# Four blocks of 32 columns in place of two of 64, in the stretches of an FFN loop that have no convolution pairs beside them

## The chip, the cores and the metric

The kernel runs on one core of one Trainium2 chip. The metric is device time in microseconds (us) from one launch; three runs of the kernel before gave a median of 2205.84 us (2205.76 to 2206.69). All arithmetic is in fp32.

## What is computed

A long convolution by FFT, a multiplication, and a feed-forward network (FFN) with a maximum of three products. Cut to what matters:

```python
h_filt = (np.maximum(pos_emb @ w1, 0.0) @ w2) * np.exp(-0.01 * pos)[:, None]
u = x * v                                          # (4, 12544, 128)
Uf, Hf = np.fft.rfft(u, n=2 * S, axis=1), np.fft.rfft(h_filt, n=2 * S, axis=0)
y = np.fft.irfft(Uf * Hf[None], n=2 * S, axis=1)[:, :S]
t = (x * y).reshape(4 * 12544, 128)
h = np.maximum(np.maximum(t @ m1, t @ m2), t @ m3) # m1, m2, m3: 128 x 768
out = h @ m_out                                    # 768 x 128
```

## The kernel before

**Stages.** A prologue builds the filter's spectrum and the convolution of batch 0 (it ends near 284 us of the span). Then a main loop (lines 1264 to 1311) runs the FFN of batches 0, 1 and 2 and, beside it, the convolution of the next batch. A last stage (from line 1320, near 1792 us) runs the FFN of batch 3 with a Strassen-like scheme and nothing beside it.

**Tiles and slots.** A batch is 32 tiles of 392 tokens (4 positions by 98), and each tile takes 6 slots, one for each block of 128 of the 768 hidden columns. The main loop therefore has 3 x 192 = 576 slots. A slot issues, in this order: `up` (line 844, two products of a 128x128 weight block with 392 columns of tokens, each evicted by ScalarE or VectorE), perhaps `t_sums`, `down` of two slots before (line 855, one product, and one more with `lin` at the first block of a tile), in one slot of a tile `t_last` (line 825, the last stage of the inverse FFT of the next tile: eight products of 49 columns with a weight of 90 rows), and then `run(besides...)`, the steps of the next batch's convolution that the planner put in this slot. Line 1309 issues one `t_last` more near the end of the loop.

**The products' blocks.** `up`, `down` and `t_last` all go through `halves_mm` (line 164). It cuts the 128 columns of the stationary operand into blocks of `block[0]` columns, one matmul to each, and each block writes its own partitions of the output. `block` is 64 at line 162 and is set to 32 at line 1317, ahead of the last stage. So the main loop runs two blocks of 64 and the last stage four blocks of 32. In the trace, each fp32 matmul is two instructions (two passes), so a product of 392 columns is 4 MATMUL instructions with blocks of 64 and 8 with blocks of 32. The passes are issued in the order pass 1 of all blocks, then pass 2 of all blocks.

**What runs beside.** Two kinds of step of the next batch's convolution use TensorE. `u_two` (line 496) is the first stage of the FFT of two units: 64 instructions at line 451, on tiles of 49 rows by 64 columns. `g_quarter` (line 539) is what the change calls pairs: its instructions at lines 549 and 559 are on tiles of 64 rows by 64 columns. Both write other shapes of the array than the FFN's 128 rows by 64 columns.

**The planner.** `conv_steps` (line 669) spreads these steps over the slots. It places the units first (line 685, every `2 * UNIT * per_pair` slots), then the pairs: pair x starts at slot `s0 + int(x // 2 * 2 * per_pair)`, with x from 0 to 47. By lines 681 to 703, `per_pair` is 2.520 for the steps beside batch 0 and 2.542 for those beside batches 1 and 2, and `s0` is 60, 59 and 59. The last pairs start at slot 175 of each batch. Units run in slots 2 to 52 of a batch, and, for the batch after next, in slots 183, 187 and 191 of batches 0 and 1. The `plan` list holds the slots of `t_sums` and `t_last` for each tile.

**Queues.** SyncE issues the loads of the units, of the pairs and of the tiles `zt`; GpSimd issues weight loads, the stores `zd` and `out_dram`, and computes the units' products and planes. VectorE multiplies the result of `t_last` (line 839) into the tile that `up` reads in the next tile's slots.

## Time and profile before

| what | value |
|---|---|
| median of three runs | 2205.84 us |
| the profiled execution, its own time | 2205.64 us |
| its span, first to last instruction | 2203.9 us |
| PE busy | 2186.5 us (99%) |
| VectorE, ScalarE, GpSimd busy | 70%, 55%, 54% |
| mean granted TensorE clock | 0.999 |

"PE" is TensorE's matmuls, "PEld" its weight loads. The ends of matmuls are modelled, so in the timeline the starts are what counts: the distance from the start of one group to the start of the next is what the group takes on TensorE. A line of the timeline gives the start in us, the length, engine, source line, operation, the tiles' names (output from inputs), the array tile as rows*columns, the moving operand's size, and how many instructions were merged. Line 169 is the helper `halves_mm`, so the kind of product is read from the names: `hps<-gt,w_sb` is `up`, `ops<-hid,wo_sb` is `down`, `ops<-gt,lin` the product with `lin`, and `cps<-f4p` (`last<-f4p` in the last stage) is `t_last`.

### The profile page before, as it was taken

To read this page: it belongs to the slowest core of one execution; us is meant where nothing else is said; L and a number is where in the kernel's file an instruction comes from. 1 tells how busy PE (TensorE), PEld (TensorE's weight loads), DVE (VectorE), ACT (ScalarE), POOL (GpSimd) and SP (SyncE) were. 2 spreads that over 40 slices of the span, in tenths; PEclk is the share of its full clock that TensorE was granted. 3 is DMA by queue.
4 is the path that set the end of the run, shared out by engine and by line. 5 is a ranking of instruction groups with operands and counts; after the bars stand their busy time and mean duration, and the time that the engine had idled before them with its cause. 6 is when DMAs were issued, how large, how long until landed. Compare 5 with 4: busy or idle time off the path is not lost.

```text
span 2203.9 us, 77207 instructions
## 1 busy us (share of the span) xinstructions
PE 2186.5 (99%) x31655; PEld 1258.5 (57%) x31655; DVE 1533.7 (70%) x3292; ACT 1211.4 (55%) x2223; POOL 1183.3 (54%) x1580
## 2 busy tenths in 40 slices
PE   9999999999999999999999999999999999999998
PEld 8988855555555555555555455555555545555565
DVE  5688966678888766668888766668878745454443
ACT  3699845466666555466666555456666522222222
POOL 1166568545544667535455566534545326666665
PEclk9999999999999999999999999999999999999999
DMA  8789999879999899789999899879999622222221
GB/s 200 184 262 318 302 181 206 170 196 247 248 245 246 209 189 178 155 193 243 245 245 251 212 193 175 171 172 244 242 251 241 179 75 59 65 71 69 59 59 24
DMA packets 491270, 411.62 MB, mean 187 GB/s; under 512 B 289379, under 2 KB 407901, under 8 KB 490917
## 3 DMA queue, kind: packets, MB, share of 16 engines
q1 hardware_dynamic: 443495, 274.33, 57.5%
q0 software_dynamic: 45936, 130.43, 20.9%
q8 instruction: 249, 4.08, 0.8%
q10 hardware_dynamic: 1486, 1.93, 0.4%
q14 instruction: 104, 0.85, 0.1%
HBM read 262.85 MB, written 84.68 MB: 158 GB/s over the span
## 4 chain that ended last, share of the span: by engine, by line
PE 93%; DVE 2%; POOL 2%; issue 1%; DMA 0%; ACT 0%; POOLq 0%; ACTq 0%; DVEq 0%
PE hps L169 46%; PE ops L169 20%; PE ops L913 6%; PE cps L169 4%; PE cps L549 3%; PE cps L451 3%; PE ps L178 3%; PE cps L559 3%; PE ps L169 2%; POOL xt L640 1%; PE last L169 1%; DVE ab L647 1%; PE ps L393 1%; DVE xs L639 1%; POOL specH L640 1%
## 5 line engine op out<-in xcount | busy, mean ns | idle before, releaser
L169 PE MATMUL hps<-gt,w_sb 128*64 128x392 f32 (+1 forms) x7672 | 1151.8, 494 | 1.8 <-DVE hid L852 1.0
L849 ACT ACTIVATE hid<-hps 128x392 f32<-128x392 f32 x768 | 382.4, 498 | 745.2 <-PE hps L169 726.9
L169 PEld LDWEIGHTS hps<-gt,w_sb 128*64 128x64 f32 (+1 forms) x7672 | 413.7, 126 | 454.5 <-issue 415.9
L852 DVE TENSOR_TENSOR hid<-hid,hps 128x392 f32<-128x392 f32 x768 | 428.5, 558 | 339.9 <-PE hps L169 321.4
L169 PE MATMUL ops<-hid,wo_sb 128*64 128x392 f32 x2304 | 476.8, 492 | 0.0
L601 POOL TENSOR_TENSOR cb<-cb,xs 128x512 f32<-128x512 f32 x135 | 178.2, 1320 | 358.3 <-DVE xs L598 349.8
L169 PEld LDWEIGHTS ops<-hid,wo_sb 128*64 128x64 f32 x2304 | 165.7, 137 | 213.5 <-issue 213.5
L574 DVE TENSOR_TENSOR cb<-cps,eo 128x512 f32<-128x512 f32 (+1 forms) x288 | 175.2, 650 | 78.0 <-ACT eo L571 76.9
L867 POOL DMA_DIRECT2D out_dram<-ot x96 | 77.1, 803 | 263.6 <-ACT ot L865 247.3
L589 ACT ACTIVATE xs<-cb 32x512 f32<-32x512 f32 x270 | 169.5, 628 | 21.9 <-DVE cb L574 13.1
L590 ACT COPY xs<-cb 32x512 f32<-32x512 f32 x270 | 166.3, 616 | 3.1
L605 DVE TENSOR_TENSOR xs<-cb 128x256 f32<-128x256 f32 x270 | 148.3, 598 | 7.3 <-POOL cb L601 7.3
L431 ACT COPY uT<-turned 113x512 uint16<-113x512 uint16 x180 | 125.9, 770 | 1.9 <-DMA turned<-planes 1.7
L388 POOL TENSOR_TENSOR ut<-ut 128x392 f32<-128x392 f32 x90 | 92.8, 1032 | 43.1 <-DMA ut<-in_vr_dram 42.9
L582 POOL DMA_DIRECT2D zd<-cb x135 | 93.8, 695 | 39.9 <-DVE cb L574 36.8
L169 PEld LDWEIGHTS cps<-f4p,even 90*64 90x64 f32 x1552 | 87.2, 138 | 35.9 <-issue 33.1
L777 POOL DMA_DIRECT2D xT<-in_x_dram x172 | 101.4, 605 | 4.6 <-DVE ab L647 3.1
L473 DVE TENSOR_TENSOR low<-high,cps 128x180 f32<-128x180 f32 x186 | 54.7, 336 | 68.9 <-ACT high L463 68.9
L938 POOL DMA_DIRECT2D out_dram<-o x120 | 72.6, 610 | 45.6 <-DVE o L931 44.5
L169 PE MATMUL cps<-f4p,zt 90*64 90x49 f32 x1552 | 95.9, 222 | 0.0
L415 POOL COPY planes<-ut 128x392 uint16<-128x392 uint16 x180 | 94.9, 561 | 0.0
L169 PE MATMUL cps<-f4p,even 90*64 90x49 f32 x1552 | 94.6, 220 | 0.0
(173 smaller groups left out, 3306.1 us busy)
## 6 DMA issues: line engine op xcount, KB each, us to landing
ht<-hd SPq DMA_DIRECT2D x264, 256.0 KB, 6.8
wt<-wq_const POOLq DMA_DIRECT2D x144, 256.0 KB, 5.6
zd<-cb POOLq DMA_DIRECT2D x135, 256.0 KB, 5.1
zt<-zd SPq DMA_DIRECT2D x384, 90.0 KB, 3.8
sq<-spec SPq DMA_DIRECT2D x528, 64.0 KB, 5.9
ut<-in_xr_dram SPq DMA_DIRECT2D x128, 196.0 KB, 4.0
ut<-in_vr_dram SPq DMA_DIRECT2D x128, 196.0 KB, 4.3
wt<-wt_const SPq DMA_DIRECT2D x90, 256.0 KB, 5.1
```

The lines of the kernel that those rows point to most:

```text
L169: nc.tensor.matmul(out[h:h + w], lhsT[:, h:h + w], rhs, start=start, stop=stop, skip_group_check=True)
L415: nc.gpsimd.tensor_copy(w[:, h, :, :, 0:HB], a[:].bitcast(U16).rearrange("p s (m e h) -> p h s e m", e=2, h=2)[:, h])
L431: nc.scalar.copy(uts[u][0:HR, 8 * (u % 2):8 * (u % 2) + 8].rearrange("n s r t -> n (s r t)").bitcast(U16).rearrange("n (s r t h) -> n h s ...
L574: nc.vector.tensor_tensor(out=cb[:, a, lo:hi], in0=ps[:, lo:hi], in1=eo[:, lo:hi], op=op)
L589: nc.scalar.mul(xs[at:at + 32], xt[at + 32:at + 64], -1.0)
L590: nc.scalar.copy(xs[at + 32:at + 64], xt[at:at + 32])
L601: nc.gpsimd.tensor_tensor(out=xts[g], in0=xts[g], in1=xs[:], op=ALU.add)
L605: nc.vector.tensor_tensor(out=ab[:, q], in0=y[:, 0], in1=y[:, 1], op=(ALU.subtract, ALU.add)[q])
L777: eng.dma_start(xT[c * NG:(c + 1) * NG].rearrange("d i p n -> d (i p) n"), x[:, 4 * i:4 * i + 8, c, b, :])
L849: nc.scalar.activation(h[:], pa[:, 0:N], Relu)
L852: nc.vector.tensor_tensor(out=h[:], in0=h[:], in1=pb[:, 0:N], op=ALU.max)
L913: nc.tensor.matmul(ps[32 * q:32 * q + 32, 0:H2], w[:, m:m + 32], rhs[:, H2 * c:H2 * c + H2], start=start, stop=True, skip_group_check=True)
```

## The change

`conv_steps` also returns the slot two after the start of the last pair, which is 177 in all three batches, and the main loop sets the block size anew in each slot. Slots 0 to 59 (0 to 58 in batches 1 and 2) and 177 to 191 run `up`, `down` and `t_last` in four blocks of 32 columns; the slots between stay at two of 64. The last value is 32, so the first `up` of batch 3 and the two `down` after the loop (lines 1313 to 1315) also go to 32. The last stage had 32 already. The steps of the units and pairs do not use `halves_mm` and keep their shapes.

```diff
-        return slots, plan, s0
+        return slots, plan, s0, start(NK + LATE - 1) + 2
...
-            plan, pairs_from = plans[b]
+            plan, pairs_from, pairs_to = plans[b]
...
         for f in range(NF):
-
+            block[0] = 64 if pairs_from <= i * NF + f < pairs_to else 32
             if i < NT - 2:
```

## The prediction

> **What bounds the kernel now.** I read the page first, then TensorE's waits in the stretches that the change touches, then busy time by stretch, then the timeline. The page says that TensorE is the bound and carries the chain:

> ```profile
> PE 2186.5 (99%) x31655; PEld 1258.5 (57%) x31655; DVE 1533.7 (70%) x3292; ACT 1211.4 (55%) x2223; POOL 1183.3 (54%) x1580
> ...
> PE 93%; DVE 2%; POOL 2%; issue 1%; DMA 0%; ACT 0%; POOLq 0%; ACTq 0%; DVEq 0%
> ```

> A busy PE is modelled, so I asked for TensorE's waits in 290 to 436 us and 1740 to 1792 us, two stretches without pairs: none is listed in either. What counts there is the distance between starts, and a time saved on TensorE is saved in the span as long as the others keep up. Busy time by stretch (us, with instructions; clock, DMA share, GB/s at the end) for a stretch without pairs, one of the prologue and one of the last stage:

> ```profile
> 300.00:440.00 140.00, 140.00 (x1800) 72.76 (x1798) 91.78 (x271) 75.37 (x140) 96.37 (x144) 1.00 1.06 191
> 130.00:210.00 80.00, 80.00 (x1698) 71.41 (x1696) 71.30 (x190) 77.66 (x142) 53.54 (x70) 1.00 0.95 312
> 1860.00:1890.00 30.00, 30.00 (x596) 15.27 (x592) 13.87 (x26) 7.61 (x16) 20.84 (x25) 1.00 0.21 54
> ```

> In the first stretch GpSimd, the busiest of the others, has 96 of 140 us. The DMA engines are full there, which matters for a rival.

> The last stage already runs blocks of 32, so the trace shows both sizes. A stretch without pairs, in blocks of 64:

> ```profile
> 305.67 0.29 PE L169 MATMUL cps<-f4p,zt 90*64 90x49 f32 x4
> 305.79 1.50 PE L169 MATMUL hps<-gt,w_sb 128*64 128x392 f32 x8
> 307.12 0.83 PE L169 MATMUL ops<-hid,wo_sb 128*64 128x392 f32 x4
> 307.88 1.48 PE L451 MATMUL cps<-f1e,uT 49*64 49x90 f32 x64
> 309.29 1.54 PE L169 MATMUL hps<-gt,w_sb 128*64 128x392 f32 x8
> 310.66 0.83 PE L169 MATMUL ops<-hid,wo_sb 128*64 128x392 f32 x4
> ```

> The border of the two sizes, and `t_last` in blocks of 32:

> ```profile
> 1790.71 1.49 PE L169 MATMUL ops<-hid,wo_sb 128*64 128x392 f32 x8
> 1792.13 6.79 PE L169 MATMUL hps<-gt,w_sb 128*32 128x392 f32 x80
> 1798.74 0.27 PE L169 MATMUL last<-f4p,even 90*32 90x49 f32 x8
> ...
> 1822.55 0.27 PE L169 MATMUL last<-f4p,even 90*32 90x49 f32 x8
> 1822.64 0.27 PE L169 MATMUL last<-f4p,zt 90*32 90x49 f32 x8
> ...
> 1823.26 1.50 PE L169 MATMUL hps<-gt,w_sb 128*32 128x392 f32 x16
> 1824.58 0.52 PE L913 MATMUL ops<-hid,tw 128*32 128x196 f32 x8
> ```

> **The change, part by part.** How much is touched: 60 + 15 slots beside batch 0 and 59 + 15 beside batches 1 and 2 make 223 of 576. A `t_last` stands in slot 2, 3 or 4 of each tile; tiles 0 to 9 and 29 to 31 of a batch lie in those slots (13), times 3, and one more from line 1309: 40. Products of 392 columns: 223 x 3, one with `lin` for each of 12 tiles a batch (36), and 4 after the loop: 709. Visits to the units' products (line 451): all 46 lie in those slots.

> *`up` and `down`.* From the border on, 80 instructions are 5 `up`, or 10 products, in 1798.74 - 1792.13 = 6.61 us: 0.661 each, with what the switch costs in it. In blocks of 64, a slot without anything else takes 1.97 to 1.98 us in the timeline (1761.58, 1763.55, 1765.53), 0.658 a product. Single passes stand 329 ns apart in either size. The four blocks start a few ns apart and then stream side by side, as the two do. I take no difference. The upper end is the last stage's slot, one `up` and two half products in 1.98 us, or 0.660 a product: 709 x 0.0017 = 1.2 us lost. The lower end is 0: both sizes stream the same 392 columns twice.

> [...]

> *`t_last`.* In blocks of 64 it takes 0.92 us (timeline: 293.40 to 294.32, 1744.04 to 1744.96, 1756.69 to 1757.61), and the `up` behind it 1.33 (305.79 to 307.12) where an `up` otherwise takes 1.316. A product of 49 columns takes 0.115 us (305.67 to 305.79). In blocks of 32 it is 0.088 us, the whole `t_last` 0.71 (1822.55 to 1823.26; 0.70 at 1798.74 and 1905.73), and the `up` behind it 1.32. [...] The saving is 0.92 - 0.705 + 0.015 = 0.23 us, times 40 = **9.2 us**. Its input `zt` is ready without a wait on TensorE now, and `up` of that tile comes at least one slot later, so VectorE's multiplication at line 839 hides as before.

> *Switches of shape.* At the border the two `down` (1.316 us) should end at 1792.03, and the first `up` in 32 starts at 1792.13: 0.10 us. Five `up` then take 6.61 where 5 x 1.316 = 6.58: 0.03 more. So a switch from 64 to 32 costs about 0.13. The way from 64 to the units' tiles costs the same 0.10 (307.12 + 0.66 = 307.78, start at 307.88), and behind the units the `up` takes 1.37 (309.29 to 310.66), 0.05 over its due. The change adds one switch 64 to 32 and one 32 to 64 in each batch, and takes away the one at 1792.13: 3 x (0.13 + 0.15) - 0.13 = **+0.7 us**.

> *Units beside blocks of 32.* Each of the 46 visits now goes from 32 to 49x64 tiles and back. No row shows that pair of shapes. The switches in the rows above cost 0.10 to 0.13, whatever the two shapes, so I take the same for the way in. For the way back I take the 0.03 of the border in place of 0.05: 46 x -0.025 = **-1.1 us**. Bounds: -46 x 0.05 = -2.3 if the way back lost its extra; +46 x 0.10 = +4.6 if one more stall of the border's size came with each visit.

> *More instructions.* A slot gets 12 more MATMUL and as many weight loads, a `t_last` 32 and 32: 223 x 24 + 40 x 64 = 7,900 on top of the program's 77,207. I cost this at nothing: the prologue row above feeds TensorE 3,394 instructions in 80 us (42 a us) at a DMA share of 0.95 with PE busy throughout. The 300 to 440 stretch goes from 3,598 to some 5,500 (55 slots of 24 and 9 `t_last` of 64 more), 39 a us. If that cover is gone it is a rival.

> Sum: -9.2 + 0.7 - 1.1 + 0 = -9.6 us. The profiled execution, 2205.64 us with a span of 2203.9, becomes 2196.0; it lies 0.2 under the median of 2205.84, so the median becomes **2196.2 us** (-0.44%).

> **The rivals.**

> *A, slower: leaving and entering four column tiles is dear.* There are 92 switches between 32 columns and the units' tiles. From 0.10 us extra at each, the gain is gone (9.6 / 92); at 0.2 extra, one and a half times the dearest switch of the rows (0.13), they cost 18.4 us and the time is 2205.8 - 9.6 + 18.4 = 2214.6. For it: no row has this pair of shapes. Against it: three kinds of switch have one price. [...] 0.11.

> *B, slower: the instruction feed.* The feed shares the DMA engines, whose share is 1.06 in the stretch. It decides if TensorE is fed under 39 instructions a us. At 36, each such stretch of 140 us would need 5,500 / 36 = 153, and 3 of them cost some 40 us: 2245. Against it is the prologue's row. 0.03.

> *C, no change: the gain is given back as waits.* The units' transposes and loads fill the DMA engines, and GpSimd waits 15.4 us for `ut` loads in 290 to 440. If TensorE were paced by them, 2205.8. Against: TensorE shows no wait there, and the loads are issued up to 9 slots ahead, against a saving of 2.3 us in a stretch of 60 slots. 0.10.

> *D, a part of the gain:* the bounds of products and units fall to the dear side, or a product pays for starting two more blocks. With +1.2 for the products and +4.6 in place of -1.1 for the units: 2205.8 - 9.2 + 0.7 + 1.2 + 4.6 = 2203.1. With the border's 0.661 for every product (0.003 more, 2.1 us) and the rest as forecast: 2198.3. 0.12 in all, spread from 2198 to 2203. [...]

> **How the numbers follow.** My forecast has 0.64, within 2194.3 (the way back loses its extra, and a little more) to 2199. Its own range and D's to 2203.1 hold 0.76; to hold 0.8 the range goes a little into C, 2194.3 to 2205. A measurement can tell about 0.2% from no change, here 2201.4 to 2210.3. Faster by more: 0.64 and most of D, 0.73. Within: C, the rest of D and the mild half of A, 0.16. Slower: the rest of A, and B, 0.11.

> **What would show it.** In the profile after, `t_last` before 440 us should be rows of 90*32 with x8, 0.70 to 0.71 us from its first start to the next `up`; slots without side work should still take 1.97 to 1.98; the way from `down` to line 451 should still lose 0.10 and the `up` behind it take 1.34 to 1.37. The first pair of batch 0, at 441.65 us now, should come 2.3 us earlier (10 x 0.23), and the last stage some 9 us earlier. The prediction is wrong if the visits to line 451 take longer, if TensorE's weight loads wait for issue at the slots' starts, or if waits for VectorE or a DMA appear on TensorE in those stretches.

## The result, and the profile after

The changed kernel takes 2209.12 us (median of 20 runs, 2205.29 to 2215.47); the kernel before, on the same chips, 2206.98 (20 runs, 2205.30 to 2209.60). The ratio is 1.0013, 95% interval 1.0007 to 1.0019: not 9.6 us faster but some 3 us slower, outside the stated range. The runs also spread more than those of before. The profiled execution is the slowest of the 20 (2215.47 us, span 2213.7), so its account is not that of a typical run.

The page of the changed kernel, where it answers to the lines of before:

```profile
PE 2187.1 (99%) x35763; PEld 1267.0 (57%) x35763; DVE 1535.4 (69%) x3292; ACT 1213.1 (55%) x2223; POOL 1188.7 (54%) x1580
...
q8 instruction: 281, 4.60, 0.9%
...
PE 91%; POOL 3%; DVE 2%; issue 2%; DMA 2%; ACT 1%; POOLq 0%; SPq 0%; ACTq 0%; DVEq 0%
```

TensorE's busy time is the same, but its idle time grew from 2203.9 - 2186.5 = 17.4 us to 2213.7 - 2187.1 = 26.6, and the chain has a second percent of "issue", time in which an engine waits for nothing that the profile shows. Queue q8, of the kind `instruction`, moved 281 transfers; before it moved 249 (`q8 instruction: 249, 4.08, 0.8%`).

Where the time went is seen by cutting the span at the first and last instruction of each batch's pairs (lengths in us, from the starts in the traces; "free" is a stretch without pairs: free 0 from the first `up`, free 1 and 2 from the last pair of one batch to the first of the next; the 2 to 4 us ahead of the first `up` are left out; e3, e6a and e6b are told below):

```
                         before    after     e3    |   e6a     e6b
up to the first t_last   281.56   284.02   284.42  |  282.56  282.96
free 0                   157.73   165.19   157.94  |  157.73  155.99
pairs 0                  304.70   306.32   315.06  |  304.47  304.47
free 1                   196.35   197.34   196.62  |  196.51  193.73
pairs 1                  306.76   306.52   307.30  |  306.53  306.54
free 2                   196.35   193.65   196.62  |  196.49  193.74
pairs 2                  306.03   306.03   313.00  |  307.00  306.03
rest of batch 2           46.91    45.98    47.04  |   46.91   45.98
last stage               405.12   405.08   405.18  |  405.18  405.16
```

Free 2 went nearly as forecast, 2.70 us shorter, and so did the rest of batch 2. Free 0 is 7.5 us longer.

Not all of the 9.8 us between the two spans can be put down to the change. The 2.5 us ahead of the first `t_last` lie in code that is the same in both, and other kernels here with that same code took 281.6 to 284.4 for it. From there to the first `up` another 1.2 us came in, and behind it the granted clock is at 0.50 from 287 to 293 us, which makes the time from the first `up` to the next `t_last` 10.97 us in place of 9.48. This half clock comes without the change too: e3, with blocks of 64 in free 0, has it there, and so has e13 (told below), which is the kernel before up to the last stage:

```profile
287.00:290.00 3.00, 3.00 (x12) 1.22 (x10) 2.90 (x10) 0.58 (x2) 1.47 (x2) 0.50 0.79 199
```

The 1.6 us of pairs 0 hold one wait of 1.2 us for the input `sq` of a pair (at 691 us), in slots whose blocks are 64 in both kernels. Some 3 us are left for the rest of the loop. TensorE's timeline in free 0, changed kernel:

```profile
425.50 0.27 PE L169 MATMUL cps<-f4p,zt 90*32 90x49 f32 x7
426.73 0.23 PE L169 MATMUL cps<-f4p,zt 90*32 90x49 f32 x1 [0.97 <-issue]
426.74 0.31 PE L169 MATMUL cps<-f4p,even 90*32 90x49 f32 x8
...
429.39 1.31 PE L451 MATMUL cps<-f1e,uT 49*64 49x90 f32 x55
433.49 0.71 PE L451 MATMUL cps<-f1e,uT 49*64 49x90 f32 x9 [2.78 <-issue]
434.13 2.72 PE L169 MATMUL hps<-gt,w_sb 128*32 128x392 f32 x16
```

TensorE stops in the middle of a product: after 7 of 8 instructions of a `t_last` that need nothing but what the seven had, and after 55 of 64 of the units' products. No input can be late there. And the `up` behind the second stop takes 2.55 us instead of 1.32. The windows around it (us, TensorE's busy time and instructions first, then its weight loads, VectorE, ScalarE, GpSimd; granted clock, DMA share, GB/s at the end) say why:

```profile
424.00:430.00 6.00, 5.03 (x137) 2.64 (x133) 2.48 (x7) 0.99 (x2) 2.82 (x3) 1.00 1.06 239
430.00:434.00 4.00, 1.22 (x47) 0.96 (x36) 1.29 (x4) 0.46 (x1) 0.00 (x0) 0.90 0.62 168
434.00:437.00 3.00, 3.00 (x25) 0.91 (x24) 0.00 (x1) 0.96 (x2) 0.00 (x0) 0.57 0.02 5
```

After the stop the granted clock is 0.57. TensorE's waits in 290 to 442 us of the changed kernel, in total, times, longest; of before, none was listed there:

```profile
PE cps L451 <- issue: 2.8, 1, 2.8
PE cps L169 <- issue: 1.3, 2, 1.0
PE hps L169 <- issue: 1.1, 1, 1.1
```

**The instruction feed in the trace.** Before, TensorE ran 63,310 matmuls and weight loads; with the 601 instructions that wait for semaphores or drain, which are counted from here on, that is 63,911. Queue q8 has 249 transfers of 16 KB there, one for every 257, and the 8,216 that the change adds go with 32 more, again one for every 257. So I take q8 for TensorE's instructions, and a transfer for 256 of them. I set the start of each transfer against the count of TensorE's instructions started by then. In all profiles of this case, from 20 us on, no transfer n started before TensorE was 150 instructions past 256 n, and TensorE was never further than 449 past it before transfer n had landed. I read this as a store of instructions: a load is due at 150, and at 449 the store is empty. No view shows the store itself; the two counts are what was measured. Between them lie 299 instructions, and the time that they take is the time that a load has. Of the six gaps over 0.7 us between two instruction starts from 290 to 1800 us of the changed kernel, five stand at just this place (instruction 193 of a 256, 449 = 256 + 193), and TensorE went on 1.5 to 1.7 us after the transfer's end; the sixth is the wait for `sq`. Before has none there. Because of these 1.5 us a load cost time here also where it landed before the store was empty: of the five, two landed 0.03 and 1.55 us after that moment, the other three 0.4 to 0.9 us ahead of it. The times from due to landed, against the time in which TensorE uses up 299 instructions (us):

```
                            landed median / longest    store median / shortest
before, 288 to 440               3.07 / 8.31                11.38 / 10.56
after, 288 to 440                4.47 / 7.60                 7.89 /  4.33
before, prologue 130 to 210      3.93 / 5.37                 6.98 /  6.84
before, 1800 to 2195             1.94 / 3.43                 6.66 /  5.50
```

The longest landing and the shortest store need not belong to the same load, so each load has to be set against its own 299 instructions. With blocks of 64 in the main loop of before the closest load landed 3.5 us before its store was empty, and in the prologue 1.6 us (130 to 210). In the changed main loop seven landed with less than 1 us left or after it. The changed kernel uses up the store fastest where a `t_last` in blocks of 32 (64 matmuls and 64 weight loads in 0.70 us) stands near the units' products (128 in 1.41): 256 of the 299 are gone in 2.1 us.

### The profile page after: what moved, and what is told of

Read it like the earlier page. It is cut to its first block, busy times and chain, and to the rows that moved or that the text cites. A ratio compares the mean times of both kernels' runs of the same rounds, so it can differ in the third digit from the quotient of the medians.

```text
span 2213.7 us, 85423 instructions
## 1 busy us (share of the span) xinstructions
PE 2187.1 (99%) x35763; PEld 1267.0 (57%) x35763; DVE 1535.4 (69%) x3292; ACT 1213.1 (55%) x2223; POOL 1188.7 (54%) x1580
## 4 chain that ended last, share of the span: by engine, by line
PE 91%; POOL 3%; DVE 2%; issue 2%; DMA 2%; ACT 1%; POOLq 0%; SPq 0%; ACTq 0%; DVEq 0%
PE hps L169 46%; PE ops L169 20%; PE ops L913 6%; PE cps L169 4%; PE cps L549 3%; PE cps L451 3%; PE ps L178 3%; PE cps L559 3%; POOL xt L640 1%; PE ps L169 1%; PE last L169 1%; DVE ab L647 1%; PE ps L393 1%; DMA zt<-zd 1%; DVE xs L639 1%
## 5 line engine op out<-in xcount | busy, mean ns | idle before, releaser
L169 PE MATMUL hps<-gt,w_sb 128*32 128x392 f32 (+1 forms) x9464 | 1168.8, 496 | 2.5 <-issue 1.7
L169 PEld LDWEIGHTS hps<-gt,w_sb 128*32 128x32 f32 (+1 forms) x9464 | 420.2, 118 | 456.4 <-issue 412.7
L169 PE MATMUL ops<-hid,wo_sb 128*32 128x392 f32 (+1 forms) x3196 | 488.0, 492 | 0.0
L169 PEld LDWEIGHTS ops<-hid,wo_sb 128*32 128x32 f32 (+1 forms) x3196 | 162.7, 122 | 219.6 <-issue 218.8
L169 PEld LDWEIGHTS cps<-f4p,even 90*32 90x32 f32 (+1 forms) x2192 | 82.6, 121 | 37.5 <-issue 33.7
L593 DVE TENSOR_TENSOR cb<-cb,ht 128x512 f32<-128x512 f32 x135 | 92.1, 682 | 1.8 <-ACT xs L590 1.6
L598 DVE TENSOR_TENSOR xs<-xs,ht 128x512 f32<-128x512 f32 x135 | 92.0, 682 | 0.0
```

The source lines that it names most:

```text
L169: nc.tensor.matmul(out[h:h + w], lhsT[:, h:h + w], rhs, start=start, stop=stop, skip_group_check=True)
```

## The experiments

Theory F: TensorE uses up its instructions faster than they land. Rivals: N, the number of instructions costs by itself, wherever; K (and B32), blocks of 32 cost through clock, weights or switches.

**e1 and e2: the turning transfers left out**, at 64 and at 32. Both leave out the turning of the units, so the FFT's data of batches 1 to 3 is another.

```diff
-        nc.sync.dma_start_transpose(
-            out=t[:], in_=us.pop(u)[:].rearrange("p h s n -> p (h s n)"))
+        nc.sync.dma_start(out=t[:], in_=us.pop(u)[:].rearrange("p h s n -> p (h s) n"))
```

> This kernel has blocks of 64 as before, and leaves out the turning of the units: the DMA transposes at line 422 become plain copies of the same bytes, so the FFT of batches 1 to 3 gets unturned data. It is the base for the next kernel. Theory F (feed): in the changed kernel TensorE runs out of instructions, because their loads stand behind the transposes on full DMA engines; here, at blocks of 64, there is hardly such a stall, so the time stays within 4 us of before (2203 to 2208), and the DMA share near 300 to 440 us falls from 1.06 to under 0.6. Rival N (number alone: four blocks cost by their number of instructions, whatever the DMA engines do): the same here. Rival K (clock: blocks of 32 lower the granted clock): the same here.

> The changed kernel (32 where no pairs run) with the same left out: plain copies in place of the transposes. F: with the DMA engines free the instructions come in time, so no wait of TensorE for issue over 0.3 us is left between 290 and 1800 us, and the gain that the working of t_last gives comes through: 8 to 10 us less than e1_no_turn_64. N and K: 0 to 4 us more than e1_no_turn_64, as the change itself showed, and stalls or a lower clock remain.

Measured: 2208.45 (ratio to before 1.0005, 0.9997 to 1.0014) and 2203.96 (0.9988, 0.9979 to 0.9997): 4.5 us in favour of 32, where the change itself lost 2 to 3. That is against N and K, but half of what F expected. e2 still has four gaps at the store's end (0.73 to 1.37 us): its DMA share in 300 to 440 us is 0.78 (e1: 0.76, not under 0.6), and loads there still land up to 7.2 us after they are due.

**e6a and e6b: most of the units' transfers left out**, at 64 and at 32: no turning transfer, and one of a unit's two inputs (it is multiplied with itself).

```diff
-        for src in (xr, vr):
+        for src in (xr, vr)[:1 if b else 2]:
...
-        nc.sync.dma_start_transpose(
-            out=t[:], in_=us.pop(u)[:].rearrange("p h s n -> p (h s n)"))
-        us[u] = t
+        us[u] = us[u][:].rearrange("p h s n -> p (h s) n")
```

> Base for the next kernel: blocks of 64, and most of the units' transfers left out in batches 1 to 3: no turning transfer at all (the join reads the planes as they are), and only one of the two loads of a unit (it is multiplied with itself). Both theories: near before, 2202 to 2207.

> The changed kernel with the same transfers left out. F: the loads of instructions land sooner than in e2_no_turn_32, so more of the gain comes through, 7 to 10 us less than e6a_light_64 against 4.5 us between e2_no_turn_32 and e1_no_turn_64. B32: the same as that 4.5 us or less, since transfers do not matter.

Measured: 2207.83 (0.9994, 0.9985 to 1.0003) and 2199.44 (0.9965, 0.9951 to 0.9978), a difference of 8.4 us: nearly the whole gain that the prediction saw. The same 300 to 440 us, e6a and then e6b:

```profile
300.00:440.00 140.00, 140.00 (x1800) 72.77 (x1798) 91.21 (x270) 75.68 (x141) 91.25 (x144) 1.00 0.47 108
```

```profile
300.00:440.00 140.00, 139.68 (x2778) 66.74 (x2772) 91.78 (x271) 76.17 (x141) 92.63 (x144) 1.00 0.49 112
```

With the DMA share at half, e6b feeds 5,550 instructions in 140 us with 0.3 us of stop, and has no gap at the store's end over 0.7. From 288 to 440 us its loads land after 2.5 us in the median, against 4.5 in the changed kernel; the latest takes 7.2 us here too, but it met a stretch whose store lasted 8.0. By stretches without pairs it gains 1.74, 2.78, 2.75 and 0.93 us. TensorE's work is the changed kernel's, form by form; what differs is transfers. So it is neither the number of instructions alone (N) nor the blocks of 32 (K, B32).

**e3: the complement, 32 only beside pairs; e4: 32 from the first pair on.**

```diff
-            block[0] = 64 if pairs_from <= i * NF + f < pairs_to else 32
+            block[0] = 32 if pairs_from <= i * NF + f < pairs_to else 64   # e3
+            block[0] = 32 if pairs_from <= i * NF + f else 64              # e4
```

> The complement of the change: blocks of 32 only in the slots with pairs beside them (351 to 353 of 576, with 57 or 58 t_last), 64 where none run. F: TensorE needs 23.5 instructions a us there now and about 32 with blocks of 32, under the 37 to 40 at which the changed kernel stalled, and no transposes run there; few stalls, so 57 x 0.23 = 13 us less for t_last, 1 us more for switches: 2193 to 2197. N: more instructions are added than by the change (351 x 24 + 57 x 64 = 12,000 against 7,900), so 2209 to 2214. K: the same sign as N.

> Blocks of 32 from the first pair of a batch to its end, 64 only in slots 0 to 59 of each batch, where most units run. F: the gain of e3_beside_pairs and 2 us more (10 t_last x 0.23), 2191 to 2195, less if the units in slots 183 to 191 of batches 0 and 1 already starve TensorE. N and K: slower than before by more than the change, 2210 to 2216.

Measured: 2224.20 (1.0072, 1.0058 to 1.0085) and 2229.44 (1.0095, 1.0083 to 1.0108). F's numbers were wrong in sign. Its rule, an average of under 37 instructions a us, was the wrong rule: beside pairs e3's loads land a median of 5.4 and up to 8.7 us after they are due (450 to 740 us), while a `t_last` and a slot's pairs (up to 64 matmuls and 64 weight loads) empty the store in as little as 4.7. TensorE's four largest waits in 284 to 1800 us of e3, and one of the stops, 6 matmuls into a pair:

```profile
PE cps L559 <- issue: 5.7, 6, 1.9
PE hps L169 <- issue: 4.5, 3, 3.2
PE ops L169 <- issue: 3.9, 4, 1.4
PE cps L549 <- issue: 3.2, 3, 1.9
```

```profile
512.15 0.44 PE L549 MATMUL cps<-sq,wt 64*64 64x128 f32 x6
514.50 0.54 PE L549 MATMUL cps<-sq,wt 64*64 64x128 f32 x9 [1.91 <-issue]
```

All 14 gaps over 0.7 us from 290 to 1800 us in e3, and 15 of 17 in e4, stand at instruction 193 of a 256. The kind of stop is F's in every one of these. N had the sign, but not the size (2209 to 2214), and e6b is against it.

**e5: as many instructions without blocks of 32.** In the slots without pairs, `up` and `down` keep blocks of 64 and are cut into halves of 196 columns.

```diff
+        m = n // 2 if split[0] and n == 4 * NB else n
+        for c in range(0, n, m):
             for h in range(0, P, w):
-                nc.tensor.matmul(out[h:h + w], lhsT[:, h:h + w], rhs, ...
+                nc.tensor.matmul(out[h:h + w, c:c + m], lhsT[:, h:h + w], rhs[:, c:c + m], ...
```

> Blocks of 64 everywhere in the main loop, but in the slots without pairs each product of up and down is cut into two of 196 columns, so that these slots issue as many instructions for it (24 more) as with blocks of 32, and no block of 32 is in it. A pass of 196 columns takes 166 ns in the last stage against half of 329, which is 6 ns a product or 4 us in all. Theory F (TensorE runs out of instructions where it uses them faster than their loads land): 4 us for the products and some 6 to 10 us of stalls for issue in the same stretches as in the changed kernel, 2215 to 2222. Rival B32 (it is the blocks of 32 themselves, by their weights, switches or clock, that cost): only the 4 us, 2209 to 2212, and no waits for issue.

Measured: 2214.66 (1.0032, 1.0021 to 1.0043), between the two. In the profiled execution the stretches without pairs are 4.8 us longer, some 4 of it the price of the halves by the estimate above, and one gap (0.9 us) stands at the store's end. `t_last` keeps its 32 matmuls here, so the store lasts 6.7 us or more. It does not decide; it fits that the bursts matter more than the mean rate.

**e7: only the 40 `t_last` at 32.**

```diff
+        w, block[0] = block[0], 32 if narrow[0] else block[0]
         for s in range(4):
...
+        block[0] = w
```

> Only the 40 t_last of the slots without pairs go to blocks of 32; up and down stay at 64. F: 2,560 more instructions in place of 7,900, so few stalls; 40 x 0.23 = 9.2 us less for t_last, and 2 switches of 0.13 more for each, 10.4 us, come to about +1: 2206 to 2210. B32 (blocks of 32 cost as such, and with them every switch): 3 to 6 us over before.

Measured: 2210.23 (1.0012, 1.0003 to 1.0020), 2.3 us over before: just past F's upper end, and under B32's 3 to 6. No gap at the store's end. Free 1, with 13 `t_last`, is 0.57 us longer than before: 0.044 each, so if a `t_last` saves its 0.23, the two added switches cost 0.23 + 0.044 = 0.27 us, 0.137 each, and eat the saving. Free 0 is 2.8 us longer in this profile for another reason: two waits for `hid` at 332 and 336 us, behind a wait of ScalarE of 3.5 us for a turning transfer. So in this one profile a late transfer of data did hold up TensorE, which is rival C's way of losing time, though not with the changed kernel's blocks.

**e8, e9, e10: transfers added to the last stage**, which runs blocks of 32 without a stop. e8 adds loads of the units' form that nothing reads; e9 adds them with blocks of 64 in that stage; e10 has the blocks of 64 alone.

```diff
+            if 12 <= step < 168:
+                for src in (xr, vr):
+                    t = inp.tile([P, 4, NB], FP32, tag="u0" if src is xr else "u1", name="junk")
+                    nc.sync.dma_start(t[:], src[...])
```

> The kernel before, with transfers added where there were few: in steps 12 to 167 of the last stage SyncE also issues two loads of 196 KB each, of the units' form, into tiles that nothing reads. The stage runs blocks of 32 as before, about 41 instructions a us, and took 405.1 us in every profile so far. F: with the DMA engines busy the loads of TensorE's instructions land later than the 5.5 to 6.6 us that its store of them lasts, so waits for issue appear in this stage, and it takes 5 to 25 us longer. Rival S (the stalls come from something in the stretches without pairs, the units' products, switches or blocks' mixture, and not from transfers and the use of instructions): the stage stays within 2 us of 405, or waits for the inputs zt appear and not for issue.

> The same added transfers, with blocks of 64 in the whole last stage (up, t_last and the half products). F: TensorE uses about 25 instructions a us there, its store lasts some 11 us, so the transfers cost under 3 us against e10_last_64 and hardly a wait for issue appears. S: the same difference between e9_traffic_64 and e10_last_64 as between e8_traffic_32 and before.

> Base for the one ahead of it: the kernel before with blocks of 64 in the last stage, no added transfers. Both theories: 30 t_last of 0.23 us more, so 5 to 8 us over before, 2211 to 2216, without waits for issue.

Measured: e8 2207.12 (0.9989, 0.9980 to 0.9999), e9 2213.84 (1.0024, 1.0015 to 1.0033), e10 2214.36 (1.0028, 1.0015 to 1.0041). The last stage took 405.07, 411.59 and 411.58 us; e10's 6.5 us more are what both theories expected. F's 5 to 25 us did not come, and rival S's figures did, though the DMA engines were full, here in e8's last stage:

```profile
1830.00:2120.00 290.00, 290.00 (x5910) 192.56 (x5901) 141.48 (x260) 75.14 (x160) 193.03 (x230) 1.00 1.06 244
```

With a DMA share of 1.06 and 244 GB/s the instruction loads land after 2.9 us in the median and 4.8 at the most. So in this stage full DMA engines by themselves did not make them late. What is left of S, that it takes something of the stretches without pairs, is answered by e6b, which has their products, switches and mixture of blocks and no stop over 0.7 us, and by e3, which stops beside pairs. The interval of e8 also shows how far an edit that costs nothing can come out from 1, about 0.1%; the change's own 1.0013 is hardly more, so its loss of 2 to 3 us is less sure than that the 9.6 us did not come.

**e11 to e14: large packets in place of small ones.** The packets in flight while a load waits (from due to the start of its transfer) differ between long and short waits: over the thirteen profiles so far, the 132 waits over 5.5 us had 63 us of packet time on q1 in packets of 2 KB and 24 on q0 in packets of 4 KB or more, in the mean; waits under 1.5 us had 0.7 and 0.9. A part of this is length alone, 6.5 us against 0.9. e11 and e12 add a load of 512 KB in rows of 4 KB each step (blocks of 32 and 64), e13 and e14 three loads at once in every fourth step.

```diff
-                for src in (xr, vr): ...
+                t = utp.tile([P, 16, 2, 32], FP32, tag="uT", name="junk")
+                nc.sync.dma_start(..., wt_d[step % NK].rearrange("p a f -> p (a f)"))
```

> As e8_traffic_32, but the added transfers of the last stage are one load of 512 KB a step in rows of 4 KB to a partition, in place of two of 196 KB in pieces of 392 bytes. Theory F2 (an instruction load of 16 KB waits for the large packets ahead of it, not for full DMA engines as such; in all profiles so far the 132 waits over 5.5 us had packets of 2 KB and more ahead of them): instruction loads land 4 to 8 us after they are due, past the 5.5 to 6.6 us that TensorE's store lasts at blocks of 32, so waits for issue appear in the last stage and it takes 3 to 30 us longer than 405.1. Rival S: as in e8_traffic_32 nothing happens, 405 to 406 us, because full DMA engines do not starve TensorE outside the main loop.

> The same added loads of 512 KB with blocks of 64 in the last stage, whose store lasts some 11 us. F2: under 3 us over e10_last_64 (its last stage took 411.6 us) and hardly a wait for issue. Rival S: the same difference as between e11_big_32 and before.

> As e11_big_32, but in every fourth step only, three loads at once (two of 512 KB in rows of 4 KB, one of 196 KB in rows of 1.6 KB), so the DMA engines are loaded in bursts and not paced to the end; blocks of 32. F2: an instruction load that falls into a burst lands after 4 to 8 us, at times past the 5.5 to 6.6 us of the store, so some waits for issue appear in the last stage and it takes 2 to 15 us over 405.1, zt hardly waits. Rival S: 405 to 407 us and no wait for issue.

> The same bursts with blocks of 64 in the last stage. F2: no wait for issue, within 2 us of the 411.6 us that this stage took in e10_last_64. Rival S: the same difference as between e13_burst_32 and before.

Measured: e11 2284.41 and e12 2272.68 us (1.0356 and 1.0297), for another reason than either theory had. The added loads hold up the inputs `zt`, as TensorE's waits in e11's last stage say, and no wait for issue is listed:

```profile
PE last L169 <- DVE even L820: 29.4, 8, 7.0
PE last L169 <- DVE even L818: 13.9, 3, 5.9
```

e13 2208.18 (1.0001, 0.9991 to 1.0010) and e14 2214.54 (1.0034, 1.0020 to 1.0049): stages of 405.14 and 411.58 us, no stop, as rival S had it; e13's loads land after 5.9 us at the most. So I could not make the loads late enough in the last stage, and what makes them land after 6 to 10 us in the main loop stays open; that it is the size of the packets ahead was not shown. In the main loop GpSimd's and SyncE's queues and the turning transfers run at once; that mixture was not rebuilt.

No version here that does the whole computation is clearly faster than the kernel before; e8's 0.1% is that of an edit which only adds transfers.

## Why the prediction was wrong, point by point

**The step that failed is "More instructions. I cost this at nothing".** It compared mean rates, 42 instructions a us in the prologue against 39, at a DMA share of 0.95 against 1.06. What decided in these traces was whether each load landed some 1.5 us before its 299 instructions were used up. In the prologue the closest load had 1.6 us left, so that row stood at the edge and was no cover for denser bursts; in the changed main loop five had 0.92 us or less and each cost a stop of 0.8 to 3.0 us. The count itself was a little low: 8,216 instructions came on top, not 7,900, mostly since the products with `lin` were left out of it. The rival that named the feed had the mechanism, at a chance of 0.03, and a wrong condition (under 39 a us) and price (2245) from the same mean.

The gain that TensorE's work allows was right: 9.6 us forecast, 8.4 measured by e6b against e6a. From the medians, 8.4 forgone and 2 to 3 lost make some 11 us of stops and slow clock in a typical run; that is worked out and not seen, since one execution is profiled. In that one, free 0 has gaps at instruction 193 of 0.56, 1.59, 1.17 and 3.02 us and 1.5 us of half clock behind the last of them, and the half clock at its start, which comes without the change too, cost 1.5. Against a gain of 2.3 that makes +7.0; measured +7.5, so some 0.4 us are not accounted for.

- `up` and `down`: right. Slots without side work take 1.98 us (1335.13, 1337.11, 1339.09) and passes stand 329 ns apart. The blocks' starts are 3 to 7 ns apart, but these do not add to the time of a product here:

```profile
1330.95 0.84 PE L169 MATMUL ops<-hid,wo_sb 128*32 128x392 f32 x8
1331.73 1.48 PE L451 MATMUL cps<-f1e,uT 49*64 49x90 f32 x64
1333.14 1.52 PE L169 MATMUL hps<-gt,w_sb 128*32 128x392 f32 x16
1334.48 0.84 PE L169 MATMUL ops<-hid,wo_sb 128*32 128x392 f32 x8
1335.13 1.50 PE L169 MATMUL hps<-gt,w_sb 128*32 128x392 f32 x16
```

- `t_last`: right, 0.70 us in blocks of 32 where no stop falls into it.
- Units beside blocks of 32: nearly right. The `up` behind them takes 1.34 us (1333.14 to 1334.48), as forecast; the way in is 0.02 dearer (0.78 us from `down` to line 451 against 0.76), so the 46 visits gave 0.5 us and not 1.1. The rival that made these switches dear is out.
- Switches between sizes: right, 0.137 us each in e7, if its `t_last` save what they were forecast to, against 0.13.
- The rival of waits for the units' inputs: TensorE's waits in 290 to 442 us list nothing but issue. (In e7 two such waits came.)
- "The first pair 2.3 us earlier, the last stage 9 us earlier": both came later, 452.8 against 441.65 and 1808.6 against 1798.7.

## What to carry to other kernels

Before you cut an engine's work into more instructions, find how fast it uses up its instructions in its densest few microseconds, and set that against the times from due to landed of its instruction loads there, load by load and with a margin (1.5 us here), not against a mean rate. Here the stops were gaps in the middle of runs of like instructions with "issue" as their releaser, and nearly all at one instruction number modulo 256: 193 for five of the six over 0.7 us in the changed kernel's main loop, for 14 of 14 in e3 and for 15 of 17 in e4. The saving of 0.23 us a `t_last` was not worth it where it was paid with bursts of instructions beside dense transfers: 9.6 us forecast, 2 to 3 lost.

## What the runs showed of the hardware

Behind the stop of 3.0 us in the changed kernel's free 0 the granted clock was at half. It had fallen before TensorE went on at 433.49 us, and the products behind the stop lost some 1.5 us by it:

```profile
433.20:436.50 3.30, 3.01 (x25) 1.23 (x29) 0.00 (x0) 0.96 (x2) 0.00 (x0) 0.50 0.03 11
```

The clock was at half there after some 2.5 us without an instruction (from 430.71, the modelled end of the last one), and the gaps of 1.1 and 0.8 us at 801 and 937 us left it at 1.00. In e3 a longer stop, 3.16 us idle up to 1514.40, left it at 1.00 too:

```profile
1510.00:1515.00 5.00, 1.84 (x18) 0.51 (x14) 2.90 (x5) 1.12 (x2) 3.01 (x4) 1.00 1.05 268
```

So in these traces the length of a gap alone does not tell whether the clock fell; what else decided is not shown.
